# Fourth gate tile folded into the free rows of the other three, decays over a whole unit, and unit 0's scans ahead of its inverses, in a fused recurrence-and-FFN kernel

## Chip, cores and metric

One core of one Trainium2 chip. The metric is device time in microseconds (us) of one launch; the median over several launches is quoted. "Faster" and "slower" mean by more than 2%.

## The reference, cut

```python
# batch 4, heads 8, seq 768, head_dim 48; d_model 384, d_ff 2048
f = 1.0 / (1.0 + np.exp(-f_logit))
for t in range(S):
    state = f[:, :, t, :, None] * state + np.einsum('bhd,bhe->bhde', k[:, :, t], v[:, :, t])
    y[:, :, t] = np.einsum('bhd,bhde->bhe', q[:, :, t], state)
# x = y as (batch*seq, 384)
h = x @ w_in
g = np.where(h > 0.0, h, np.exp(np.minimum(h, 0.0)) - 1.0)
out = g @ w_out
```

The logits have mean 2 and deviation 0.5, so `f` is near 0.88.

## The kernel before

The 3072 tokens are 12 **units** of 256 (three to a batch). In each unit the recurrence becomes matmuls: with G the running product of 1/f, `k` is multiplied by G and `q` by its inverse. The plain `q`-`k` product (the *scores*), masked, gives the part inside 64-token chunks; a 48x48 *state* for each head carries the rest. The result `x` goes into the *up-projection* (x by w_in), the ELU, and the *down-projection* (by w_out). TensorE interleaves one unit's projections with the next unit's recurrence. Unit 0 has nothing to hide behind: that is the start of the kernel.

Heads go two to a tile of 128 rows. Two heads of 48 need 96 rows (16 to 111), so rows 0 to 15 and 112 to 127 of each tile are blank. A unit has four such tiles (`HP = 4`) for each of f, k and q; `NKT = 3`.

```python
qkf = [{n: cst.tile([128, HP, U], FP32, name=f"{n}{i}") for n in "fqk"} for i in range(NB)]
# ... cut ...
def decays(u, p):                       # once for each of the four tiles of a unit
    t = qkf[u % NB]
    g = t["f"][:, p]
    for c in range(1 if u or p else NC):
        a = g if u or p else g[:, c * C : (c + 1) * C]
        nc.vector.tensor_tensor_scan(   # running product, restarted at each 64-token chunk
            out=a, data0=a, data1=restart[:, p] if u or p else a, initial=1.0, op0=ALU.mult, op1=ALU.max
        )
    nc.vector.reciprocal(pts[u][:, p], g)
    nc.gpsimd.tensor_tensor(out=t["k"][:, p], in0=t["k"][:, p], in1=g, op=ALU.mult)
    # ... q by pts: tiles 0 to 2 on GpSimd, tile 3 on VectorE ...

def step(u, c):                         # one chunk of the state: a sum AND a product
    # ... cut ...
    if u % UPB or c:
        nc.vector.tensor_tensor(out=s, in0=now, in1=sts[u, c][:]..., op=ALU.add)
        now = s
    nc.vector.tensor_tensor(out=s, in0=now, in1=decay, op=ALU.mult)
```

The start (unit 0), in program order; in the traces every engine runs its instructions in this order (VectorE in before: scans at 9.24, 11.57 and 13.90 us, each with its reciprocal behind it). `warm(n)` is n filler matmuls that only keep TensorE busy:

```python
warm(5)
for p in range(HP):
    decays(0, p)
    if p % 2:
        transposed(0, p // 2, f"m{p // 2}")
    if p < HP - 1:
        warm(2)
# ... scores, state sums, mask, first half of the outputs, fetches of weight slices 2 to 6 ...
split(1); decays(1, 0); first_outputs(1); warm(2); lower(1); decays(1, 1)   # joined lines, two cut
at_step(0, lambda: decays(1, 2))
at_step(1, lambda: decays(1, 3), lambda: watch(1))
at_step(4, lambda: warm(4))
attention(1, (), A1)
```

`split`, `lower` and `merge` turn a loaded weight slice into the form that TensorE reads, on VectorE, ScalarE and VectorE again.

## Time and profile before

| | before |
|---|---|
| median, lowest, highest (3 runs) | 574.97, 574.79, 575.47 us |
| span of the traced execution | 574.7 us |
| first up-projection starts | 31.14 us |
| first down-projection starts | 49.58 us |
| reciprocals on VectorE | 48, 84.1 us |

A row of a timeline reads: start, duration (us), engine, source line, operation, output<-inputs, sizes, count, and in brackets how long the engine had stood idle and what ended that ("issue": nothing that the profile shows). The *granted clock* is the share of its full clock that TensorE was given; the *DMA share* is the mean busy share of the 16 DMA engines. The same operations stand at other lines before and after:

| role | before | after |
|---|---|---|
| filler | L981 | L1024 |
| scores | L660 | L701 |
| sums for the states | L681 | L724 |
| first unit's outputs | L760 | L804 |
| up- / down-projection, first units | L880 / L910 | L923 / L953 |
| state sum / product (VectorE) | L644 / L647 | L682 / L687 |

The prediction shows the main lines. TensorE's timeline inside the first half of unit 0's outputs, one loop of 48 equal matmuls:

```profile
21.37 0.42 PE L760 MATMUL psY<-at,padded_v 64*32 64x64 f32 x15
24.03 1.11 PE L760 MATMUL psY<-at,padded_v 64*32 64x64 f32 x33 [2.24 <-issue]
```

It stops for 2.24 us in mid-loop, and the bracket names no other engine's work. And TensorE, then VectorE, around the scores of a later unit:

```profile
322.79 0.39 PE L835 MATMUL psH<-xt,wi 128*128 128x128 f32 x2
323.10 0.32 PE L660 MATMUL psS<-q,k 64*64 64x64 f32 x2
323.63 1.15 PE L660 MATMUL psS<-q,k 64*64 64x64 f32 x62 [0.20 <-DVE state L644]
```

```profile
322.82 0.36 DVE L647 TENSOR_TENSOR state<-state,p 128x192 f32<-128x192 f32 x1
323.22 0.36 DVE L644 TENSOR_TENSOR state<-psU_a,state 128x192 f32<-128x192 f32 x1
```

Two scores go out at 323.10 and the other 62 only at 323.63, after VectorE's last state sum. The bracket counts 0.20 us; the start times show 0.53, of which the first two matmuls need a few hundredths (all 64 take 1.16 us in after).

### The profile page before, as it was taken

To read this page: it belongs to the slowest core of one execution; us is meant where nothing else is said; L and a number is where in the kernel's file an instruction comes from. 1 tells how busy PE (TensorE), PEld (TensorE's weight loads), DVE (VectorE), ACT (ScalarE), POOL (GpSimd) and SP (SyncE) were. 2 spreads that over 40 slices of the span, in tenths; PEclk is the share of its full clock that TensorE was granted. 3 is DMA by queue.
4 is the path that set the end of the run, shared out by engine and by line. 5 is a ranking of instruction groups with operands and counts; after the bars stand their busy time and mean duration, and the time that the engine had idled before them with its cause. 6 is when DMAs were issued, how large, how long until landed. Compare 5 with 4: busy or idle time off the path is not lost.

```text
span 574.7 us, 15339 instructions
## 1 busy us (share of the span) xinstructions
PE 555.7 (97%) x6236; PEld 505.4 (88%) x6236; DVE 436.1 (76%) x838; ACT 235.1 (41%) x437; POOL 273.7 (48%) x568
## 2 busy tenths in 40 slices
PE   6798999999999999999999999999999999999994
PEld 2556777778999999999999999999999999999994
DVE  7989469865896896896896897787888878845542
ACT  3376665533443433443343343442343353333331
POOL 7520015951465465366366257257357347325332
PEclk9899999999999999999999999999999999999998
DMA  8998690041032224224215206206206202201001
GB/s 207 234 242 228 178 241 0 2 117 58 2 79 74 79 68 113 77 59 116 83 36 140 84 10 165 84 9 166 83 7 168 86 3 60 84 2 35 29 1 35
DMA packets 36432, 50.93 MB, mean 89 GB/s; under 512 B 3552, under 2 KB 27136, under 8 KB 36352
## 3 DMA queue, kind: packets, MB, share of 16 engines
q1 hardware_dynamic: 35872, 49.56, 32.6%
q8 instruction: 51, 0.84, 0.6%
q10 hardware_dynamic: 480, 0.30, 0.2%
q14 instruction: 29, 0.24, 0.1%
HBM read 44.04 MB, written 4.72 MB: 85 GB/s over the span
## 4 chain that ended last, share of the span: by engine, by line
PE 82%; DVE 8%; DMA 3%; ACT 2%; issue 2%; POOL 1%; SPq 1%; DVEq 0%; ACTq 0%; POOLq 0%
PE psH L835 30%; PE psM L932 29%; PE psM L910 7%; PE psH L880 6%; DMA area<-in_moe_w_out_dram 2%; PE psS L660 2%; PE psY L696 2%; PE psY L716 2%; PE psT L628 1%; PE psU_a L681 1%; DVE state L644 1%; DVE state L647 1%; DVE hh L857 1%; DVE u43h L857 1%; DVE o L942 1%
## 5 line engine op out<-in xcount | busy, mean ns | idle before, releaser
L835 PE MATMUL psH<-xt,wi 128*128 128x128 f32 (+1 forms) x960 | 177.1, 293 | 0.0
L899 POOL TENSOR_TENSOR sums<-gg 128x128 f32<-128x128 f32 x160 | 69.7, 456 | 180.4 <-DVE gg L889 139.0
L867 ACT ACTIVATE gg<-hh 128x512 f32<-128x512 f32 x80 | 50.5, 631 | 223.7 <-POOL sums L899 132.0
L835 PEld LDWEIGHTS psH<-xt,wi 128*128 128x128 f32 x960 | 135.9, 192 | 0.8
L835 PE MATMUL psH<-xt,area 128*128 128x128 f32 x640 | 110.5, 275 | 0.0
L835 PEld LDWEIGHTS psH<-xt,area 128*128 128x128 f32 x640 | 96.8, 191 | 4.1
L932 PE MATMUL psM<-area,sums 128*128 128x192 f32 x480 | 91.1, 326 | 0.0
L844 DVE TENSOR_TENSOR hh<-psH,u 128x256 f32<-128x256 f32 x80 | 33.6, 420 | 69.9 <-ACT u L842 69.9
L609 DVE RECIPROCAL p<-f 128x256 f32<-128x256 f32 x48 | 84.1, 1753 | 1.7
L932 PEld LDWEIGHTS psM<-area,sums 128*128 128x128 f32 x480 | 80.2, 190 | 0.0
L932 PE MATMUL psM<-wo,gg 128*128 128x192 f32 x320 | 68.1, 335 | 0.0
L868 ACT ACTIVATE gg<-gg 128x512 f32<-128x512 f32 x96 | 60.6, 631 | 3.0
L889 DVE SCALAR_TENSOR_TENSOR gg<-gg,hh 128x512 f32<-128x512 f32 x80 | 56.5, 706 | 1.5 <-ACT gg L868 1.5
L932 PEld LDWEIGHTS psM<-wo,gg 128*128 128x128 f32 x320 | 50.2, 190 | 1.9
L857 DVE TENSOR_TENSOR hh<-psH,u43h 128x256 f32<-128x256 f32 (+1 forms) x160 | 49.6, 352 | 2.7
L899 POOL TENSOR_TENSOR sums<-gg,sums 128x128 f32<-128x128 f32 x80 | 43.4, 542 | 6.3
L610 POOL TENSOR_TENSOR k<-k,f 128x256 f32<-128x256 f32 x48 | 35.5, 740 | 21.4 <-DVE f L606 19.2
L880 PE MATMUL psH<-xt,wi 128*128 128x256 f32 x192 | 44.6, 382 | 0.0
L910 PE MATMUL psM<-wo,gg 128*128 128x384 f32 x128 | 44.2, 488 | 0.0
L880 PEld LDWEIGHTS psH<-xt,wi 128*128 128x128 f32 x192 | 35.9, 190 | 7.0 <-issue 0.5
L899 POOL TENSOR_TENSOR sums<-sums,gg 128x128 f32<-128x128 f32 x80 | 40.0, 500 | 0.0
L857 DVE TENSOR_TENSOR u43h<-psH,hh 128x256 f32<-128x256 f32 x80 | 33.5, 419 | 7.8 <-PE psH L835 7.7
(101 smaller groups left out, 758.0 us busy)
## 6 DMA issues: line engine op xcount, KB each, us to landing
area<-in_moe_w_out_dram SPq DMA_DIRECT2D x8, 768.0 KB, 10.1
again<-in_moe_w_in_dram SPq DMA_DIRECT2D x16, 384.0 KB, 4.2
again<-in_moe_w_out_dram SPq DMA_DIRECT2D x16, 384.0 KB, 3.6
f<-in_f_logit_dram SPq DMA_DIRECT2D x12, 384.0 KB, 4.8
k<-in_k_dram SPq DMA_DIRECT2D x12, 384.0 KB, 5.8
q<-in_q_dram SPq DMA_DIRECT2D x12, 384.0 KB, 6.8
v<-in_v_dram SPq DMA_DIRECT2D x12, 384.0 KB, 7.2
area<-in_moe_w_in_dram SPq DMA_DIRECT2D x8, 576.0 KB, 9.7
```

Of the source, the lines that this page charges most:

```text
L609: nc.vector.reciprocal(pts[u][:, p], g)
L610: nc.gpsimd.tensor_tensor(out=t["k"][:, p], in0=t["k"][:, p], in1=g, op=ALU.mult)
L835: nc.tensor.matmul(to, lhsT=lhs, rhs=rhs, start=(n == 0), stop=True, skip_group_check=True)
L844: add = lambda to, x, y: nc.vector.tensor_tensor(out=to, in0=x, in1=y, op=ALU.add)
L857: add = lambda to, x, y: nc.vector.tensor_tensor(out=to, in0=x, in1=y, op=ALU.add)
L867: nc.scalar.activation(g[:], h, AF.Relu, scale=-1.0)
L868: nc.scalar.activation(g[:], g[:], AF.Exp, scale=-1.0)
L880: nc.tensor.matmul(ph[:, i], lhsT=wi[j][:, kt, i * 128 : (i + 1) * 128], rhs=xts[m][:, kt, :], start=(kt == 0), stop=(kt == NKT - 1),)
L889: nc.vector.scalar_tensor_tensor(out=g[:], in0=g[:], scalar=-1.0, in1=phs.pop(P), op0=ALU.add, op1=ALU.max)
L899: nc.gpsimd.tensor_tensor(out=s[:, i], in0=x, in1=y, op=op)
L910: nc.tensor.matmul(pm[t][:], lhsT=g[:, i, t * 128 : (t + 1) * 128], rhs=wo[:, 2 * j + i, :], start=(j == 0 and i == 0), stop=(j == NP - 1 ...
L932: nc.tensor.matmul(pm[bank][:, half * DH : (half + 1) * DH], lhsT=x, rhs=y, start=first, stop=(j == NP - 1), skip_group_check=True,)
```

## The change

The intent: VectorE has 76% busy time and reciprocals of 1.75 us are its dearest single item, so give it a quarter fewer; and let unit 0 reach the first projections sooner.

- The fourth tile's 96 rows of logits are loaded into the 32 blank rows of the other three `f` tiles. One scan and one reciprocal a unit fall away; two small transfers (`move`) bring the results back into tile 3.
- The running product is kept over the whole unit (limit 2^80 instead of 2^60), so a state step is one sum, with one product at a unit's end.
- Unit 0: all scans ahead of all inverses; unit 1's scans ahead of unit 0's mask; one weight slice is fetched later in the order; 4 filler calls for 17.
- Blank rows of x are filled by two transfers instead of six.

```diff
-    qkf = [{n: cst.tile([128, HP, U], FP32, name=f"{n}{i}") for n in "fqk"} for i in range(NB)]
+        {n: cst.tile([128, HP, 2, U] if n == "f" else [128, HP, U], FP32, name=f"{n}{i}") for n in "fqk"}
@@ load
+            if n == "f":
+                to, frm = to[:, 0:NKT, 0], frm[:, 0:NKT]
+            for r in range(2 if n == "f" else 0):
+                nc.sync.dma_start(
+                    out=qkf[u % NB][n][GAP[r] : GAP[r] + PAD, 0:NKT, 0], in_=src[n][b, 2 * NKT + r, ...]...)
@@
+    def grow(u, p):
+        g = qkf[u % NB]["f"][:, p, 0]
+        nc.vector.tensor_tensor_scan(out=g, data0=g, data1=g, initial=1.0, op0=ALU.mult, op1=ALU.max)
+    def fall(u, p):
+        nc.vector.reciprocal(f[:, p, 1], f[:, p, 0])
+    def move(u, which, queue):
+        for r in range(2):
+            to = PAD + D * r
+            queue.dma_start(out=f[to : to + D, NKT, which], in_=f[GAP[r] : GAP[r] + PAD, 0:NKT, which])
@@ step
-        nc.vector.tensor_tensor(out=s, in0=now, in1=decay, op=ALU.mult)
+        if c == NC - 1:
+            nc.vector.tensor_tensor(out=s, in0=s, in1=end, op=ALU.mult)
@@ start, cut
-    warm(5)
+    warm(W0)                      # W0 = 3
+    for p in range(NKT):
+        grow(0, p)
+        scale(0, ("k", p, nc.gpsimd))
+    move(0, 0, nc.scalar)
+    fall(0, 0)
+    warm(WA)                      # WA = 1
+    pc = scores(0, ("m2", "m3"), (0,))
+    fall(0, 1)
+    scale(0, ("k", NKT, nc.gpsimd), ("q", 1, nc.gpsimd))
+    fall(0, 2)
+    move(0, 1, nc.scalar)
+    # ... rest of unit 0's scores, unit 1's bias and scans, masks, states, split(0), fetches ...
+    first_outputs(0)
+    lower(0)
+    merge(0)
+    first_outputs(1)
-    warm(2)
-    at_step(4, lambda: warm(4))
```

## The prediction

The 1753 ns are those of a reciprocal of 128x256. 574.7 - 7.0 = 567.7, less some 0.3 of later idle time, came to 567.5 us. The 3 to 4 us for a row move are the allowance over the median of 2.9 us of before's six, an estimate, as are the issues of 0.5 us (before's six took 4.05 us, 0.68 each). "Cold" is a granted clock of 0.50. For "twice their time" in rival B the traces have 1.7 times: 36 matmuls of the outputs took 1.54 us at 0.50 in after, and 0.91 at 1.00 in e1 below.

> **What bounds the kernel now.** I read the page first, then the busy time by stretches, then each engine's timeline of the first 60 us.
>
> ```profile
> PE 555.7 (97%) x6236; PEld 505.4 (88%) x6236; DVE 436.1 (76%) x838; ACT 235.1 (41%) x437; POOL 273.7 (48%) x568
> ...
> PE   6798999999999999999999999999999999999994
> ...
> DVE  7989469865896896896896897787888878845542
> ```
>
> The last two lines are slices, 14.4 us each. TensorE is full from the fourth slice on; the empty places are in the first three. (VectorE's row is there only to show that it is full at the start as well.) The stretches say where that change lies; columns are stretch, length, busy PE, PEld, DVE, ACT, POOL, granted clock, DMA share, GB/s:
>
> ```profile
> 0.00:14.00 14.00, 9.27 (x19) 3.82 (x20) 10.35 (x17) 4.06 (x8) 10.67 (x35) 1.00 0.87 206
> 14.00:31.00 17.00, 14.10 (x312) 9.42 (x311) 15.73 (x24) 7.83 (x13) 8.81 (x19) 0.80 0.97 240
> 31.00:49.60 18.60, 15.28 (x182) 11.17 (x180) 16.00 (x27) 12.82 (x13) 2.61 (x4) 1.00 1.06 246
> 49.60:128.00 78.40, 78.40 (x663) 57.53 (x661) 58.01 (x81) 44.24 (x58) 30.37 (x59) 1.00 0.43 114
> 128.00:568.00 440.00, 438.69 (x5067) 423.46 (x5065) 335.13 (x691) 166.18 (x347) 221.20 (x454) 1.00 0.25 68
> ```
>
> From 49.6 to 568 us TensorE idles 1.3 us in all. So VectorE, ScalarE or GpSimd work saved per unit after 49.6 is worth nearly nothing. What can move the end is the time at which the first down-projection (the x8 group at 49.58) starts. From there to the end are 574.7 - 49.6 = 525.1 us, which the change leaves alone: same matmuls, same tail. TensorE's timeline of the stretch before, last bracket what it waited for:
>
> ```profile
> 28.46 2.85 PE L981 MATMUL psW<-ident 128*128 128x512 f32 x4
> 31.14 2.75 PE L880 MATMUL psH<-xt,wi 128*128 128x256 f32 x12
> 33.73 0.82 PE L628 MATMUL psT<-ident,k 128*128 128x128 f32 x6
> 35.81 0.44 PE L628 MATMUL psT<-ident,k 128*128 128x128 f32 x2 [1.25 <-POOL k L610]
> 36.08 2.76 PE L880 MATMUL psH<-xt,wi 128*128 128x256 f32 x12
> 38.67 3.60 PE L981 MATMUL psW<-ident 128*128 128x512 f32 x8
> 42.20 1.15 PE L681 MATMUL psU_a<-v,kn 64*64 64x48 f32 x64
> 43.28 2.86 PE L880 MATMUL psH<-xt,wi 128*128 128x256 f32 x12
> 47.60 0.30 PE L660 MATMUL psS<-q,k 64*64 64x64 f32 x2 [1.46 <-issue]
> 48.50 1.16 PE L660 MATMUL psS<-q,k 64*64 64x64 f32 x62 [0.60 <-DVE state L644]
> ```
>
> The first up-projection starts at 31.14. Real work to the first down is then three ups (7.8), transposes (0.85), state updates (1.1) and scores (1.1), 10.9 us; it took 18.4. The 7.6 us over are filler matmuls (3.5), a wait for GpSimd's scaled k (1.25) and about 2.5 for VectorE's state steps, which themselves stood behind a weight transfer: the chain of waits has one piece of 14.30 us for it, from 29.34 to 43.65.
>
> ```profile
> L609 DVE RECIPROCAL p<-f 128x256 f32<-128x256 f32 x8 | 14.0, 1753 | 0.3
> L606 DVE TENSOR_TENSOR_SCAN f<-f,restart 128x256 f32<-128x256 f32 x7 | 4.6, 663 | 0.0
> L542 DVE TENSOR_SCALAR bits<-area 128x768 int32<-128x768 int32 x6 | 3.9, 643 | 1.9 <-DMA area<-in_moe_w_out_dram 1.9
> ```
>
> These are VectorE's three costliest groups up to 49.6 us (count, busy us, mean ns, idle before). Eight reciprocals are 14 us of it. DMA is full too, 240 GB/s.
>
> [...]1753 ns, while a product of the same 128x256 takes 425 on VectorE. [...]after the pause from 21.8 to 24.0 the granted clock is 0.50 until 30 us. [...]The trace: six 16 KB row moves took 4.05 us to issue on ScalarE's queue, and a median of 2.9 us to land.
>
> **The change, part by part.**
> *Fourth pair folded into the free rows.* Per unit one exp/bias share, one scan (0.66) and one reciprocal (1.75) go from VectorE, 2.4 us; in units 0 and 1, 4.8 us. Added: moves of the results back into the fourth tile, two transfers each for the scan and the reciprocal in units 0 and 1. I allow 3 to 4 us from issue to landing, as DMA is full there.
> *Decays over the whole unit.* The restart copies go; a state step is one add (0.36) in place of add and product, and one product ends the unit: 5 small operations for 8, 3 x 0.43 = 1.3 us less before the scores of unit 1.
> *Order.* Scans first, so k and the transposes come before the reciprocals; unit 1's scans and one reciprocal stand before unit 0's mask. Filler falls from 17 calls to 4.
> *Blank rows* of f need no memset, so its load issues at about 0.75 us, not 1.56. Two small gap transfers follow it.
> *Gap rows* in two transfers for six: later than 49.6, worth nothing.
>
> *Working, with before's durations and after's order of instructions.* f has landed at about 4.7. ScalarE gives pair 0 at 5.6; VectorE's scans end at 6.3, 7.5, 8.2 and its reciprocals at 9.9, 11.6, 13.4. The move of the inverse lands at about 17.3 (two issues of 0.5, then 3); GpSimd scales the last q by 18.1, scores end at 18.7. Meanwhile VectorE has done unit 1's bias, scans and one reciprocal (13.4 + 0.8 + 3 x 0.66 + 1.75 = 17.9) and two steps. Masks end at 20.0, against 20.5 before: only half a microsecond. The first half of the outputs (96 matmuls, cold at first) ends near 23; two copies; ScalarE's 1.94 us weight cleaning now stands *behind* them, to 25.9, and the second half runs beside it. The copies of x (1.45) end at 27.4: first up at **27.4**, 3.7 earlier than before, of which 1.1 is filler that stood in the way.
>
> Then ScalarE and VectorE set the pace. ScalarE: copies of k (1.15) to 28.6, cleaning of the second weights to 30.5; VectorE's merge to 31.5; so the second up is at 31.5 to 34.1, 1.5 us late; state updates to 35.2. VectorE goes on: two splits (1.15 each), elu (0.65), merge at 35.6; third up 35.6 to 38.2. Then split, merge, split, elu (1.15 + 0.95 + 1.15 + 0.7) to 39.5, five steps (2.0) to 41.5. The scores need their banks: 41.5 to 42.6. **First down at 42.6** for 49.6, 7.0 earlier.
>
> Will the weights be there? The fetches behind the first two go out when GpSimd has cleared the area, at about 19.3 for 24.3. One block is 0.79 MB, 3.2 us at 245 GB/s, and the wo2 block that went ahead of all others now goes behind five. I get landings of the third to sixth blocks near 27, 30.5, 34 and 37, each just before its split. Sum: 574.7 - 7.0 = 567.7, and some 0.3 of the 1.3 us idle later may go: **567.5 us**.
>
> **The rivals.**
> *A: The row moves bind.* The trip through DMA takes the place of the fourth reciprocal. If a move takes 6 us, not 3, in a DMA that is full to 1.0, the fourth q and mask come 3 us later, and all behind them. For it: loads of 384 KB took 5 to 8 us in that stretch. Against: ScalarE's queue has nothing else in it. Then 570 to 571.
> *B: Cold clock and pauses in TensorE.* With 13 filler calls gone TensorE is cold in unit 0, and the outputs take twice their time; the 2.24 us pause in mid-group at 21.8 (put down to issue, cause not shown) may come again or move. Then first up at 29.5 and 569.5 to 570.
> *C: Everything after the first up keeps up.* If splits never wait and steps come in early, the second and third up and the scores follow without gaps: 27.4 + 10.0 = 37.4, and 562.5. Against: VectorE's own queue of 8 us of work there has no slack.
> *D: The saved VectorE work counts all along the kernel.* Ten units times some 4 us would be 7%. Against: 1.3 us of idle in 518.
> *E: The general path.* If growth over 256 tokens passed the limit, the time would multiply. Logits of mean 2 give 256 x 0.195 = 50 doublings, an estimate from the inputs, and the limit allows 80.
>
> **Range and chances.** A and B cost 2 to 4 us each and may add; C gives at most 5. So 562.5 to 572 should hold it 8 times in 10. Faster by over 2% needs under 563.5, nearly all of C: 0.18. Slower by over 2% needs a new stall of 18 us: 0.02. Within 2%: 0.80.
>
> **What would show it.** Right: the first down near 42.6; from there TensorE full; the rest 525 us; first up near 27.4; masks ending near 20; VectorE's reciprocals at 3 a unit; the scores before the first down waiting for the state steps. A is right if the last q's product waits for f's move past 20 us; B if the granted clock is 0.5 through the outputs or a pause ends in "issue"; C if the first down is under 39. The prediction fails if TensorE has gaps after 50 us (then the moves or a weight transfer hold it), or if the matmuls from the first down to the end do not take 525 us.

## The result

| | before | after |
|---|---|---|
| median, lowest, highest (4 runs each) | 574.88, 574.56, 575.47 us | 571.84, 571.39, 572.74 us |
| traced span | 574.7 us | 569.7 us |
| first up-projection | 31.14 us | 31.83 us |
| first down-projection | 49.58 us | 46.55 us |
| lead of after at 128 us / at 457 us (same group of both) | | 2.94 / 5.06 us |

The ratio is 0.9948, 95% interval 0.9931 to 0.9965: the same within 2%, 3.0 us less, where 7.4 had been forecast. Ratios here are the mean time of one kernel's fast runs over that of the other's of the same rounds, so not quite the ratio of the medians that are quoted.

The traces differ by 5.0 us and the medians by 3.0: the traced execution of before was timed at 576.45 us, above all runs in the table, and that of after at 571.39, its fastest. So the traces show *where* time moves, and medians and ratios how much.

First, what was to shrink did shrink. The page of after, busy time by engine and the reciprocals:

```profile
PE 545.2 (96%) x6210; PEld 501.2 (88%) x6210; DVE 394.5 (69%) x764; ACT 229.6 (40%) x418; POOL 266.1 (47%) x530
...
L627 DVE RECIPROCAL f<-f 128x256 f32<-128x256 f32 x36 | 62.7, 1747 | 1.3
```

VectorE lost 41.6 us of work, 21.4 of them twelve reciprocals. Second, the start. The busy time by stretches of after (columns as in the prediction):

```profile
14.00:31.00 17.00, 10.51 (x257) 8.95 (x258) 11.24 (x16) 3.60 (x7) 8.53 (x15) 0.60 1.04 254
31.00:46.55 15.55, 11.28 (x167) 8.92 (x166) 12.96 (x23) 14.26 (x15) 1.47 (x2) 1.00 0.79 202
46.55:125.00 78.45, 78.45 (x665) 57.38 (x661) 51.92 (x72) 43.18 (x54) 29.87 (x53) 1.00 0.55 143
```

VectorE's load from 14 to 31 us fell from 15.73 to 11.24 us, but TensorE's granted clock fell as well, from 0.80 to 0.60. By single microseconds it is 0.50 from 17 to 30. TensorE's timeline:

```profile
16.46 0.69 PE L665 MATMUL psT<-ident,k 128*128 128x128 f32 x2 [4.00 <-POOL k L617]
...
22.51 1.06 PE L804 MATMUL psY<-at,padded_v 64*32 64x64 f32 x29
26.32 0.85 PE L804 MATMUL psY<-at,padded_v 64*32 64x64 f32 x19 [2.74 <-issue]
27.47 1.54 PE L804 MATMUL psY<-q,state 64*64 64x64 f32 x36 [0.31 <-ACT between L810]
...
31.83 2.86 PE L923 MATMUL psH<-xt,wi 128*128 128x256 f32 x12 [0.53 <-ACT xt L816]
35.84 2.83 PE L923 MATMUL psH<-xt,wi 128*128 128x256 f32 x12 [1.15 <-DVE wi L577]
...
44.96 0.30 PE L701 MATMUL psS<-q,k 64*64 64x64 f32 x2 [2.19 <-issue]
45.47 1.15 PE L701 MATMUL psS<-q,k 64*64 64x64 f32 x62 [0.21 <-DVE state L682]
46.55 2.85 PE L953 MATMUL psM<-wo,gg 128*128 128x384 f32 x8
```

An idle stretch of 4.00 us, where fillers used to stand, then the clock at half, then the pause again: it is 2.74 us now, and inside the same loop, but after 29 matmuls of it and not 15. The first up-projection comes at 31.83, no sooner than before. From there to the first down-projection it is 14.7 us instead of 18.4.

One trace is one draw, and the start scatters. Of the experiments below, e4, e5, e11, e13 and e17 have the change's own program up to the first up-projection (but for a small memset in three). With the change they make six traces of one start: first up-projection at 29.02 to 31.83, pause from none to 2.74 us. Most differences between starts that are read from single traces below are no larger than that.

Third, the rest of the kernel. It was to stay the same; the lead grows by 2.1 us. The same scores as shown for before:

```profile
319.67 1.16 PE L701 MATMUL psS<-q,k 64*64 64x64 f32 x64
```

All 64 go out at once. VectorE's states had ended by then:

```profile
316.87 1.52 DVE L682 TENSOR_TENSOR state<-psU_a,state 128x192 f32<-128x192 f32 x4
318.42 0.36 DVE L687 TENSOR_TENSOR state<-state,f 128x192 f32<-128x192 f32 x1
```

The lead goes 3.43 at 280.5, 3.95 at 325, 4.44 at 413, 5.06 at 457 (times of before): about half a microsecond at each of these units' scores. TensorE's busy share had hidden it. In before, matmul rows overlap (322.79 + 0.39 is past 323.10), and the x2 group at 323.10 lasts 0.32 us though 64 scores together take 1.16 in after, some 0.02 each: a row's end is not the time at which TensorE could go on, and waits of a few tenths look like work. Comparing the starts of the same group in two traces finds what the busy share hides.

### The profile page after: what moved, and what is told of

It is laid out like the page before. It is cut to its first block, busy times and chain, and to the rows that moved or that the text cites. A ratio compares the mean times of both kernels' runs of the same rounds, so it can differ in the third digit from the quotient of the medians.

```text
span 569.7 us, 15171 instructions
## 1 busy us (share of the span) xinstructions
PE 545.2 (96%) x6210; PEld 501.2 (88%) x6210; DVE 394.5 (69%) x764; ACT 229.6 (40%) x418; POOL 266.1 (47%) x530
## 4 chain that ended last, share of the span: by engine, by line
PE 92%; DVE 2%; DMA 2%; issue 1%; ACT 1%; POOL 1%; ACTq 0%; DVEq 0%; POOLq 0%
PE psH L878 35%; PE psM L975 33%; PE psM L953 7%; PE psH L923 6%; PE psS L701 2%; PE psY L739 2%; PE psY L759 2%; PE psU_a L724 2%; PE psT L665 2%; ACT area L569 1%; DMA f<-f 1%; DMA k<-in_k_dram 1%; PE psY L804 1%; POOL k L617 1%; DVE bits L559 0%
## 5 line engine op out<-in xcount | busy, mean ns | idle before, releaser
L617 POOL TENSOR_TENSOR k<-k,f 128x256 f32<-128x256 f32 x48 | 39.2, 820 | 58.8 <-DMA area<-in_moe_w_in_dram 34.5
L627 DVE RECIPROCAL f<-f 128x256 f32<-128x256 f32 x36 | 62.7, 1747 | 1.3
L885 ACT COPY u<-psH 128x128 f32<-128x128 f32 x80 | 21.1, 264 | 59.3 <-PE psH L878 59.3
```

The costliest lines, as they stand in the source:

```text
L617: e.tensor_tensor(out=t[n][:, p], in0=t[n][:, p], in1=t["f"][:, p, "kq".index(n)], op=ALU.mult)
L627: nc.vector.reciprocal(f[:, p, 1], f[:, p, 0])
```

## The experiments

Each is an edit of the changed kernel unless said otherwise. All gave correct results, timed over 5 rounds beside the kernel before on the same chip (three chips in all, on which before's median was 574.7 to 575.0 us). Starts are from the traces, one for each.

| run | ratio to before, 95% | median, us | first up | first down |
|---|---|---|---|---|
| (the change) | 0.9948, 0.9931 to 0.9965 | 571.84 | 31.83 | 46.55 |
| e1_tiny60 | 0.9960, 0.9938 to 0.9982 | 571.76 | 29.97 | 45.25 |
| e2_fill4 | 0.9943, 0.9920 to 0.9965 | 571.44 | 30.20 | 45.26 |
| e3_early | 1.0383, 1.0365 to 1.0400 | 597.05 | 55.86 | 71.90 |
| e4_states8 | 0.9971, 0.9954 to 0.9987 | 573.67 | 30.88 | 47.46 |
| e5_fourth | 0.9963, 0.9948 to 0.9978 | 573.16 | 31.55 | 47.34 |
| e6_recip3 | 0.9940, 0.9918 to 0.9962 | 571.21 | 30.61 | 45.53 |
| e7_blocks | 0.9979, 0.9962 to 0.9996 | 573.49 | 31.12 | 46.23 |
| e8_all | 1.0033, 1.0010 to 1.0056 | 576.35 | 33.44 | 50.03 |
| e9_hoist | 0.9960, 0.9938 to 0.9982 | 572.33 | 32.37 | 46.57 |
| e10_hoist_fill | 0.9956, 0.9943 to 0.9969 | 572.42 | 31.59 | 46.54 |
| e11_both | 1.0023, 1.0010 to 1.0036 | 576.16 | 31.70 | 48.27 |
| e12_order_before | 1.0006, 0.9993 to 1.0019 | 575.51 | 30.50 | 48.40 |
| e13_keep2 | 0.9932, 0.9918 to 0.9947 | 570.90 | 29.02 | 44.52 |
| e14_fill_keep2 | 0.9940, 0.9922 to 0.9957 | 571.09 | 30.16 | 45.51 |
| e15_recip_fill_keep2 | 0.9940, 0.9923 to 0.9957 | 571.82 | 31.46 | 46.89 |
| e16_before_again | 0.9998, 0.9983 to 1.0013 | 575.01 | 30.52 | 48.88 |
| e17_keep3 | 0.9928, 0.9911 to 0.9946 | 571.30 | 31.13 | 45.84 |
| e18_blocks2 | 0.9948, 0.9925 to 0.9972 | 572.20 | 29.31 | 44.61 |

### The pause and the clock: e1, e2, e3

Theory (conjecture): in the pause TensorE waits for more instructions. In both traces the pause stands after exactly 221 matmuls, and a transfer of an instruction queue (q8 on the pages) begins just ahead of it (21.2 us in before, 23.4 in after). That queue makes 51 transfers of 16 KB in each of the two traces, one for some 122 matmuls (6236 in before, 6210 in after, each recorded as a weight load and a matmul). A *block* below is what one such transfer brings. The rival is something at that place of the program.

e1 adds 60 small matmuls in the idle stretch (they show as 120 records):

```diff
     pc = scores(0, ("m2", "m3"), (0,))
+    tiny(60)                 # 64x64 matmuls
```

> The changed kernel with 60 small matmuls more (64x64, results unused) in TensorE's idle stretch after the first pair's scores. Theory (the pause of 2.74 us is tied to a count of TensorE instructions: in both kernels it begins after exactly 221 recorded matmuls, at the 15th padded_v product before and at the 29th after): it begins after 221 matmuls again, so at about the 17th product of the first half of the outputs, in place of the 77th. Rival (it is tied to the place in the work or to the time, for instance to padded_v, to a full PSUM or to the DMA traffic at that moment): it stays at the 77th product or near 23.6 us. Time: the pause is only moved, so within 0.4% of the changed kernel, ratio to before 0.991 to 0.997.

e2 puts 4 full fillers (512 columns, 8 records) there instead:

```diff
     pc = scores(0, ("m2", "m3"), (0,))
+    fill(4)
```

> The changed kernel with four full-size filler matmuls in TensorE's idle stretch from 12.5 to 16.5 us. Theory (the cold clock costs about 1.5 us): the granted clock stays 1.00 through the first half of the outputs, their cadence goes from 0.036 to about 0.018 us, the pause begins 8 products earlier (after 221 matmuls in all) and stays 2 to 3 us long, then the clock may drop again; first up-projection 1 to 2 us earlier (near 30.3), ratio to before near 0.992. Rival (the pause alone holds it, a cold clock costs nothing as other waits take its place): first up-projection unchanged within 0.4 us.

e3 has small matmuls in place of the fillers, 171 calls in all:

```diff
-    warm(W0)
+    tiny(105, "m3")
@@
-    warm(WA)
+    tiny(44, "m3")           # and 16, 6 and one full one at two more places
```

> The changed kernel with its four filler calls replaced by 171 small matmuls laid ahead of the idle stretch and one filler call in it, so that the 221st matmul falls at about 12.5 us, where TensorE waits anyway. Theory: the pause moves there and costs nothing, no pause in the outputs; first up-projection 2.5 to 4 us earlier (28 to 29.3), end 2.5 to 4 us earlier than the changed kernel, ratio to before 0.988 to 0.991. Rival A (the row moves and VectorE bind, so a shorter first half only waits elsewhere): first up-projection earlier, but the first down-projection within 1 us of 46.5 and the ratio near 0.994. Rival B (every further block of instructions pauses likewise): a second pause some 128 matmuls on, and no gain.

e1's timeline of TensorE:

```profile
24.21 0.75 PE L804 MATMUL psY<-at,padded_v 64*32 64x64 f32 x37
25.92 0.41 PE L804 MATMUL psY<-at,padded_v 64*32 64x64 f32 x11 [0.96 <-issue]
```

The pause is after matmul 349 = 221 + 128 now, about one block further by the 122 matmuls of a transfer, and there is none at 221. The place that e1's expectation gave was off, as each call had turned into two records, but the count holds. Over all traces the pause stands at 221 in nine (before, the change, e4, e5, e11, e12, e14, e17, and e16, which is before again) or at 349 in two (e1, e7), nowhere else, and its size varies from 0.96 to 2.91 us. In all eleven TensorE goes on 2.6 to 3.0 us after the transfer began, however long the pause; that it waits for this transfer is read from these times and not shown otherwise. Where the loop ran later or slower (e2, e3, e6, e8, e9, e10, e13, e15, e18) there is none over 0.5 us. In the eleven the matmuls that are left of the loop last some 0.02 to 0.04 us each, and the 16 DMA engines were full (share 1.04 from 14 to 31 us in the change); whether either is the cause was not tested apart. The transfer itself took 1.2 to 1.4 us in the eleven, hardly longer than after 100 us, where DMA is nearly idle (medians of 1.0 to 1.2). What differs is when it begins: in the change 5.5 us after the matmul 128 earlier (the 93rd, at 17.88), in before 2.3. If DMA counts, it is by this wait; that the block is asked for at that matmul is not shown.

e1 also kept the granted clock at 1.00 from 17 to 31 us, against 0.54 in the change, and its first up-projection came 1.9 us sooner, which is within the scatter of the start. Its first down-projection came 1.3 us sooner, and its median is 0.1 us lower only. e2 missed its expectation: the clock fell at 21.3 us, the outputs ran at half clock, and there was no pause. So **pause and cold clock are both there in the traces, and easing both gained nothing that the time of the launch shows**. e3 was a failure as an experiment: back to back the 64x64 matmuls took 0.108 us a record, not 0.06 as in e1, and pushed the start back by 24 us. It adds only that no pause over 0.5 us came at 0.108 us a record.

### Where the later 2.1 us come from: e4, e5, e11

e4 puts a second operation (a product by ones) behind the state sums, as before had, in the eight units that do not begin a batch:

```diff
             nc.vector.tensor_tensor(out=s, in0=new, in1=old, op=ALU.add)
+        if u % UPB and c < NC - 1:
+            nc.vector.tensor_tensor(out=s, in0=s, in1=ones[:].broadcast_to([128, HP, D]), op=ALU.mult)
```

> The changed kernel with the state steps of each unit doubled again: behind each add a product by a tile of ones, so 7 or 8 operations as before the change (result unchanged). Theory (the shorter steps are worth time all along the kernel, since the scores wait for them while the matmul row still reads as busy: in the traces the lead grows from 2.94 us at 188 us to 5.06 at 457, all at the scores): it loses about 2 us after the first down-projection and about 1.3 us before it, ratio to before 0.998 to 1.001. Rival (my prediction: nothing after the first down-projection counts): only 1.3 us are lost, ratio near 0.997.

e5 puts stand-ins for the fourth tile's work back on VectorE instead, from the third unit on:

```diff
     def settle(u):
+        nc.vector.tensor_tensor_scan(out=g, data0=g, data1=g, initial=1.0, ...)   # on a spare tile
+        nc.vector.reciprocal(r, g)
         watch(u)
-        scale(u, ("q", NKT - 1, nc.gpsimd), ("k", NKT, nc.gpsimd), ("q", NKT, nc.gpsimd))
+        scale(u, ("q", NKT - 1, nc.gpsimd), ("k", NKT, nc.gpsimd), ("q", NKT, nc.vector))
```

> The changed kernel with VectorE's work on the fourth decay put back as dummies: in every unit from the third on, one scan and one reciprocal over a spare tile, and the last product of the queries on VectorE instead of GpSimd. Results stay correct. What is open: the lead of the changed kernel over the one before grows from 2.95 us at 128 us to 5.06 us at the end, in steps at the scores of each unit. Theory: the shorter queue of VectorE (one scan and one reciprocal of 1.75 us fewer a unit) lets the last state of a unit be there when the scores end. Then this kernel's lead stays at 2.9 to 3.1 us from 128 us to the end, and the time is 573.5 to 574.2, ratio 0.997 to 0.999. Rival: the growth comes from something else that the change moved (order of the products, transfers, GpSimd); then the lead grows to 5 us as in the changed kernel, time 571.5 to 572.2, ratio 0.994 to 0.9955.

e11 does both:

> The changed kernel with both dummies on VectorE: e4's second operation behind each state's sum, and e5's scan, reciprocal and last product a unit. The lead over the kernel before grew by 2.1 us after 128 us in the changed kernel and in e4, by 1.0 us in e5. Theory: it is the whole of VectorE's queue ahead of the last state that counts, so with both put back the lead grows by at most 0.5 us; time 574 to 575.2, ratio 0.9985 to 1.0005. Rival: the second half comes from something other than VectorE's amount of work (order of the scores' and products' matmuls by pair, GpSimd, transfers); then the lead grows by 0.8 to 1.1 us as in e5, time 573.2 to 574.2.

| | lead over before (first trace) at 128 us | at 457 us | growth |
|---|---|---|---|
| the change | 2.94 | 5.06 | 2.1 |
| e4, states | 0.02 | 2.16 | 2.1 |
| e5, fourth tile | 1.50 | 2.47 | 1.0 |
| e11, both | 0.85 | 0.12 | -0.7 |

Each alone gave a half answer: e4's theory fell (nothing comes back after 128 us), and e5 gave half. Together they take back all 2.1 us and 0.7 more. It is the length of VectorE's whole queue ahead of the last state that counts, and it has a threshold: the state must be there when TensorE gets to the scores. In e11 it again is not:

```profile
322.67 0.32 PE L710 MATMUL psS<-q,k 64*64 64x64 f32 x2
323.36 1.16 PE L710 MATMUL psS<-q,k 64*64 64x64 f32 x62 [0.38 <-DVE state L689]
```

The start of e11 was also 1.7 us later at the first down-projection than the change's, of which the states of unit 1 are some 1.2 (eight operations end at 46.61 instead of 45.71, begun 0.28 sooner). In time, e11's ratio is 1.0023 against 0.9948: 0.0075 of 575, or 4.3 us, more than the whole gain of 3.0. **With stand-ins for VectorE's savings put back, the changed kernel is slower than the one before.** So what the change gains it gains by VectorE's shorter queue; no gain of the new start by itself is left. Whether that start costs something is not shown: e11 is 1.3 us slower than before (0.0023 of 575), but 0.7 of this is the overshoot of the stand-ins, and its trace has the cold first down-projection that is described at e13. The stand-ins are not the removed operations to the last one, and e11 and the change were timed in different rounds, so the split is good to about a microsecond, not better.

### Is it the row move, the block, or the order of the weights: e6 to e10

e6 lets VectorE form the fourth tile's inverse itself (1.75 us), so that unit 0 waits for one row move instead of two (unit 1's first reciprocal goes behind the split for it):

```diff
-    move(0, 1, nc.scalar)
@@
     for p in range(NKT):
         grow(1, p)
+    fall(0, NKT)
```

> The changed kernel without unit 0's second row move: VectorE forms the fourth tile's decays itself with a fourth reciprocal (1.75 us), after unit 1's scans, instead of waiting for two moves of 3.7 to 3.9 us. Results stay correct. Theory A (the row moves lie on the path to the first up-projection): the last masks end 0.5 to 1 us earlier (20.0 to 20.5 instead of 21.0), the first up-projection at 30.8 to 31.4 instead of 31.8, and the time falls by 0.3 to 1 us, ratio 0.9925 to 0.994. Theory B (the path there is TensorE's own outputs, slowed by the clock of 0.50 and the pause of 2.7 us after 221 matmuls): no gain, first up-projection within 0.3 us of 31.8, ratio 0.9940 to 0.9955.

The last scores were not earlier, as the *first* move was slow in that execution (TensorE waited 4.86 us for the scaled k, not 4.00). The pause did not come, and the first up-projection was at 30.61, but for another reason than the expectation's. In the ratio, 0.9940 against 0.9948, nothing can be told apart. Rival A of the prediction, that the second row move binds, is not supported. The first move, for which TensorE waited 4.00 us in the change, was not tested apart.

e7 adds 64 recorded matmuls ahead of the outputs (I had counted 32; each filler call counts twice here too):

```diff
-    warm(W0)
+    square(24)               # 128x128 matmuls
@@
+    square(8, "m0")
+    fill(3)                  # after the first pair's scores
```

> The changed kernel with its three opening filler matmuls of 512 columns replaced by 24 of 128 columns, and 8 more such and 3 full ones in the idle gap after the first pair's scores: 32 matmuls more before the outputs. Results stay correct. Theory: [...]no pause over 0.5 us stands among the first half's outputs (20 to 27 us), nor the clock at 0.50 before them; first up-projection at 28.5 to 30.3, first down-projection at 43.5 to 45.3, time 569.0 to 571, ratio 0.990 to 0.993. Rival: the pause is tied to the place in the program (the switch from the masks to the products) or to the transfers at 23 us, not to the count; then it is seen again at 23 to 27 us and the time is within 0.7 us of the changed kernel's. If the pause goes and the time does not move, the start of the up-projection is held by something else (copies of x, split of part 1).

The pause at 221 went, as expected, and came back at 349 with 1.39 us; the clock was 1.00 but for 23.5 to 26.9 us. The first up-projection was 0.7 us sooner than the change's, and the time 1.7 us *longer* by the median. In its trace TensorE waits 1.03 us at 68.20 for unit 1's row moves of x (0.32 us in e1). More on that at e18.

e8 was a candidate with many reorderings at once:

```diff
+    move(0, 0, nc.scalar)    # ahead of the copies of k
+    split(0)
+    lower(0)                 # ahead of the outputs; unit 1's bias and scans go behind the masks; fillers as in e7
```

> A candidate that joins the lessons: the changed kernel with a fourth reciprocal in place of the second row move, the first row move issued ahead of the copies of k, the split and the lower part of unit 0 queued ahead of the outputs, more small and full fillers in TensorE's idle stretches, and unit 1's bias and scans after the masks. Results stay correct. Theory: with neither the row move nor the pause nor the clock of 0.50 in the way the first up-projection starts at 26.5 to 29, the first down-projection at 41.5 to 44, the time is 566.5 to 569.5, ratio 0.985 to 0.991. Rival: the weights' arrival and VectorE's splits of the first weight slices bound the first down-projection at 45 or later whatever the start is; then 571 or more.

It lost: with unit 1's scans behind the masks, GpSimd's scaled k of unit 1 came at 31 us, and TensorE stood 3.20 us for it ahead of the first up-projection. That speaks for putting unit 1's scans first, as the change does; with so many edits at once it is not isolated.

e9 lets the splitting of the first two weight slices start sooner; e10 is e9 with e2's fillers:

```diff
+    lower(0)
     fall(1, 1)
+    merge(0)
+    split(1)
     first_outputs(0)
-    lower(0)
-    merge(0)
+    lower(1)
     first_outputs(1)
```

> The changed kernel with only the order of the first weights' splitting moved: ScalarE's lower part of slice 0 is queued ahead of its copies between the two halves of the first outputs, VectorE's joining of slice 0 and splitting of slice 1 follow at once, and ScalarE's lower part of slice 1 comes ahead of the copies of x. Results stay correct. Theory: what sets the first down-projection is not the first up-projection but VectorE's chain of splits, which stood idle for 4.01 us until 29.37 for ScalarE's lower part and then again for 1.59 us; states of unit 1 stand at the end of that chain (43.55 to 45.7). Then the first up-projection stays at 31 to 32, the first down-projection comes at 43 to 45 instead of 46.55, time 568.5 to 570.5, ratio 0.989 to 0.992. Rival: the arrival of the first down-projection's weights, or unit 1's row moves of x at 66 to 68 us, take the gain back; then 571 to 572.

> The kernel of e9 with the 4 full filler matmuls of e2 in TensorE's idle gap after the first pair's scores. Theory: the fillers keep the clock up or move the pause as in e1 and e2, first up-projection at 29.9 to 30.6; with the splits ahead the first down-projection follows at 41.5 to 44, time 567.5 to 569.5, ratio 0.987 to 0.9905. Rival: the first down-projection hangs on the splits and the weights' arrival alone; then it is within 0.5 us of e9's, and so is the time.

VectorE in the changed kernel, one line, and then in e9, two lines:

```profile
29.37 0.96 DVE L577 CUSTOM_DVE_ANT_0 wi<-area,bits 128x1536 uint16<-128x1536 uint16 x1 [4.01 <-ACT area L569]
```

```profile
26.70 1.30 DVE L577 CUSTOM_DVE_ANT_0 wi<-area,bits 128x1536 uint16<-128x1536 uint16 x1 [0.32 <-ACT between L810]
...
36.55 0.69 DVE L932 SCALAR_TENSOR_TENSOR gg<-gg,psH 128x512 f32<-128x512 f32 x1 [2.00 <-ACT gg L911]
```

The wait of 4.01 us went, and VectorE's chain began 2.7 us sooner, but waits for ScalarE of 2.00 and 1.12 us came in its place: the states began at 43.09 instead of 43.55. The rival was right, though the thing that took the gain back was neither the weights nor x but ScalarE, which shares the chain. And e10 shows a further loss, in the first down-projection:

```profile
46.54 4.75 PE L953 MATMUL psM<-wo,gg 128*128 128x384 f32 x8
```

That group takes 2.85 us at full clock. The clock was at half again, after TensorE's gap ahead of unit 1's scores, where before had its fillers (`warm(4)`).

### The order of fetches alone, in the kernel before: e12 and e16

```diff
-    merge(0)                 # which fetched the next slice at once
+    merge(0, False)
@@
-    for n in range(2, AHEAD):
+    for n in range(2, AHEAD + 1):
```

> The kernel before with one thing changed: the weights' slice that is fetched after the first join is fetched after the other five, as in the changed kernel's order. In before VectorE waits 1.88 us for the first slice of the down-projection's weights (until 43.74) and its chain ends in the states that release the scores; in the changed kernel that wait is gone. Theory: this order alone gives back most of that wait: first down-projection at 47.4 to 48.4 instead of 49.58, time 1 to 2 us less, ratio 0.996 to 0.9985. Rival: the wait goes but VectorE's or ScalarE's work fills the time; then the ratio is 0.9985 to 1.001.

> The kernel before, unchanged, for a second trace and as a measure of the scatter: ratio 0.9985 to 1.0015, median 574.4 to 575.3. If its first down-projection comes at 49.4 to 49.8 as in the first trace, the 1.5 us by which the first trace's execution was over the median lie after it; if it comes at 48 to 48.6, they lie in the start, and the changed kernel's real lead at its first down-projection is 1.5 to 2 us and not 3.0.

VectorE's wait for w_out fell from 1.88 to 1.02 us (1.40 in the second trace of before), and the first down-projection came at 48.40; but the second trace of the *unchanged* kernel has it at 48.88, so 0.7 of the 1.2 us is scatter. In time nothing came of it (1.0006). The second trace also was of a slow execution (576.26 us, the slowest of its six runs), so where the typical run of before saves its 1.3 us is not known. Against that trace the change leads by 2.33 us at the first down-projection and 4.7 at the end. What is left of the 18.4 to 14.7 us between first up and first down is then, by exclusion, the fillers, the transposes that went ahead, and VectorE's shorter list; the order of fetches by itself is not worth a measurable amount.

### Fillers ahead of unit 1's scores, and the block boundary: e13, e14, e15, e17, e18

```diff
+        if u == 1:
+            at_step(then[3], lambda: warm(4))      # e13, e14, e15; warm(3) in e17, e18
         at_step(then[3], lambda: kept.append(scores(u)), lambda: mask(u, kept[0]))
```

> The changed kernel with 4 full filler matmuls (1.84 us at full clock) ahead of unit 1's scores, where TensorE idles 2.19 us. Results stay correct. Theory: in most executions of the changed kernel the clock falls to 0.50 after that gap and the first down-projection takes 4 us instead of 2.85; with the gap filled it stays at 1.00 from 31 us on, that group takes 2.9 us or less, the mean clock over the runs is 0.984 to 0.988, and the median is 570.8 to 571.3, ratio 0.993 to 0.994. Rival: the fillers stand in the way of the scores or the cold group was hidden by the weights' joins; then 571.6 to 572.4.

> e2 (4 full fillers in the first gap, first up-projection at 30.2 instead of 31.8, but a first down-projection of 4.49 us at the low clock) with the fillers of e13. Theory: 1.6 us of the first down-projection and about 0.4 of the scores come back, the first group is at 45.3 and takes 2.9; median 569.6 to 570.6, ratio 0.991 to 0.9925, against 571.44 of e2. Rival: as in e13; then 571.2 to 572.

> A candidate for the best: e6 (a fourth reciprocal in place of the second row move) with the fillers of e2 and of e13. Theory: no wait for the row move (2.69 us before the last scores in e2), no pause, a full clock from 30 us on: first up-projection at 29 to 30.2, first down-projection at 44 to 45.3 taking 2.9, median 569 to 570.3, ratio 0.990 to 0.992. Rival: unit 1's row moves of x or the weights hold it; then 570.8 to 571.5.

> e13 with 3 full fillers ahead of unit 1's scores instead of 4: 2.7 us instead of 3.60. Theory: with 4 they were the wait themselves (first down-projection 7.28 us after the start of the third up-projection, 6.61 in the changed kernel without them); with 3 it comes 6.6 to 6.8 us after, the clock stays at 1.00 there, the first group takes 2.85, and the median is 570.2 to 570.8, ratio 0.9915 to 0.993. Rival: the fillers' number makes no difference; 570.8 to 571.2, ratio 0.993 to 0.994. The scatter of the start (1 to 2 us from run to run) may hide it.

e14 adds e2's fillers to e13's; e15 adds both to e6. e18 is e17 with the opening fillers split up so that 32 more matmuls come ahead of the outputs, which puts the 93rd (221 - 128) ahead of the idle stretch:

```diff
-    warm(W0)
+    square(15)
@@
+    fill(4)                  # after the first pair's scores
```

> e17 with the opening fillers as 15 of 128 columns (30 recorded matmuls instead of 6) and e2's 4 full fillers in the first gap: 32 recorded matmuls more before the outputs. Theory: [...]no pause over 0.5 us in the outputs, the first up-projection at 28.5 to 29.8, the first down-projection at 43.3 to 44.6, median 569 to 570.3, ratio 0.990 to 0.992. Rival: as in e7 something else, for one unit 1's row moves of x at 66 to 68 us, takes it back; then 570.5 to 572.5.

e13's timeline of TensorE:

```profile
39.91 3.60 PE L1026 MATMUL psW<-ident 128*128 128x512 f32 x8
43.43 1.16 PE L701 MATMUL psS<-q,k 64*64 64x64 f32 x64
44.52 2.85 PE L955 MATMUL psM<-wo,gg 128*128 128x384 f32 x8
```

The four calls took 3.60 us, not the 1.84 of e13's expectation: each is two matmuls in the trace. With the fillers the clock stays at 1.00 from 31 us on and the first down-projection takes 2.85 us, in all five. Without them the traces fall in two kinds: that group was cold in nine (e2, e3, e4, e5, e6, e8, e9, e10, e11; 3.35 to 4.99 us) and warm in three (the change, e1, e7). The gaps ahead of unit 1's scores were 2.2 to 3.7 us in the nine, with a clock of 0.50 for at least a whole microsecond after them (2.19 and 2.61 us among the three). A likely reason, not tested: in before and in the change the granted clock kept each level but the last for a multiple of 3.41 us (1.00 for 17.07 and then 0.50 for 6.83 in before, 1.00 for 10.24 and then 0.50 for 13.65 in the change), and where it changed differs (23.40 and 30.23 us; 16.34 and 29.99), so a gap of some 2 us may or may not be followed by a lower clock. Four fillers were one too many (first down-projection 7.28 us after the third up-projection; 6.61 in the change and with three fillers in e17). e14 and e15 both missed their expected gain (0.9940; 0.990 to 0.9925 had been expected); in e15 TensorE waited 3.21 us for the k of the first row move. The ratios of 0.9932 and 0.9928 are the lowest of all, but each interval overlaps that of the change (0.9948), and they were timed in other rounds: better than before by 0.7% is shown, better than the change is not.

In e18 the start did what was meant: no pause, first up-projection at 29.31, first down-projection at 44.61, 1.9 us ahead of the change. Then:

```profile
67.40 2.83 PE L925 MATMUL psH<-xt,wi 128*128 128x256 f32 x12 [1.68 <-DVE wo L577]
```

and the same group in the change:

```profile
67.38 2.83 PE L923 MATMUL psH<-xt,wi 128*128 128x256 f32 x12
```

All of the lead is gone in one wait. The trace puts it down to a weight join on VectorE that this group doesn't read; in e17 and in e1 the group starts before that join has ended, so it is not the join. The group does read unit 1's x, whose blank rows come by two row moves: the last was issued at 59.7 us, took 7.4 and landed at 67.15. In e7, e1 and e15 the same wait is put down to these moves (1.03, 0.32 and 0.26 us). In the change they were issued at 60.9 and 61.5, took 6.1 and 5.6 and landed by 67.13. In e1, e7, e18 and the change alike the group starts 0.25 us after the last landing: **there is a second gate at 67 us, and the change already stands at it**. The gate is not at a fixed time: in e13 the moves took 4.4 to 4.9 us and landed by 63.9, and the lead of 2.2 us lived on to 125 us. How long these moves take goes with the DMA share in the 2 us after their issue: 4.4 to 7.4 us in the traces of this paragraph, at shares of 0.93 to 1.13, and 2.2 to 2.8 us in e4, e9 and e10, at 0.12 to 0.41. Over all traces, the 48 KB row moves of f and x took 3.2 to 8.6 us (median 5.3) where that share was above 0.9, and 2.1 to 3.0 us where it was under 0.45.

## Why the prediction was wrong

Forecast 567.5 us, measured 571.84; inside the range, but the gain was 3.0 us and not 7.4. By its own steps:

1. **"Masks end at 20.0": 21.0.** Row moves were allowed 3 to 4 us; the first took 5.1 to 5.7, the second 3.7 to 4.1. A miss of 1.0 us; 1.0 to 2.3 in the six traces of this start.
2. **"The first half of the outputs (96 matmuls, cold at first) ends near 23": 27.17. This is the term that failed.** It was given 3 us and took 6.7, of which 2.74 were the pause and most of the rest the half clock (e1, at 1.00, took 3.5 us with 0.96 of pause; 3.6 to 6.7 in the six traces, ending at 25.3 to 27.2). The prediction had both as rival B, saw them in the trace of before, and gave the pause no time in its sum although nothing in the change was aimed at it. Rival B's figure was "first up at 29.5, and 569.5 to 570"; it was 31.83. It had the direction and half the size. In before the clock had fallen to 0.50 at 23.40, after 1.6 us of the 2.24 us pause.
3. **First up-projection at 27.4: 31.83.** Of these 4.4 us, 4.2 were there at the end of the first half of the outputs (step 1 is within them); the second half and the copies, 4.4 us in the working, took 4.7.
4. **From first up to first down 15.2: 14.7.** Right, with the waits nearly where they were placed (1.15 us for VectorE's join; the state steps ahead of the scores).
5. **"VectorE, ScalarE or GpSimd work saved per unit after 49.6 is worth nearly nothing": wrong, and it hid the only gain there is.** 525.1 us from first down to end became 523.15. The reason given was TensorE's 1.3 us of idle time; with matmul rows that overlap (by 0.08 us at 323.10) that sum is no bound on the waits. Rival D was scaled wrongly (it spoke of 7%) and then dismissed with the same sum. Its size is 2.1 us after 128 us by the change's own trace; e11's stand-ins take back 2.8 there, and 4.3 us in the time of the launch, counting unit 1.
6. **The start as the only lever**: also wrong. e1 and e18 brought a first down-projection 1.3 and 1.9 us earlier and no gain in the median. e18 lost it at the gate at 67 us, which was not looked for; e1's trace kept 0.9 us to its end, which was its fastest run, and why its median shows nothing is open.

Steps 2 and 5 are errors in opposite directions, and so the total came out inside the range: that was luck. Rival A was half right (the moves are slow; e6 didn't make the second one the bound); C and E were not seen. One misreading changed nothing: TensorE's slices are full from the fifth on, not the fourth (its digit is 8).

What stays open: by how much the pause, the half clock and the row moves each delay a typical run, as the start scatters by 2.8 us from trace to trace; why both traced executions of before were 1.3 to 1.5 us slower than its typical run, and so how the 3.0 us between the medians split over the kernel.

## What to carry to other kernels

A TensorE that is 97% busy in the profile can still wait at each handover: compare the starts of the same group in two traces before calling work on another engine worthless. Fillers that are removed to "free" a start bear on the clock (from 17 to 31 us 0.54 in the change, 1.00 with e1's 60 small matmuls) and on where the pause falls (after matmul 221 in the change, 349 with e1's 120 records more), so count them as part of the design. And look for the next gate behind the one you move: here a 48 KB transfer at 67 us took back, in e18, what the start had won. Before explaining a start by one trace, take several of the same program: here they differed by 2.8 us.
